# First spread before the second group, a VectorE copy in the last four chunks, and loads and routing queued later

## The chip, the cores and the metric

The kernel runs on one core of a Trainium2 chip. A core has five engines that run side by side, each with its own queue that is worked off in order: TensorE (PE, matrix products into PSUM), VectorE (DVE), ScalarE (ACT), GpSimd (POOL) and SyncE (SP), which here only issues DMA transfers. They wait for each other through semaphores. The metric is the device time of one execution in microseconds (us), as a median of several runs.

## The reference

Two stages follow each other. The first is a delta-rule attention: 4 batches with 8 heads each, 768 steps, head dimension 48. The second is a mixture of 16 experts, chosen in two levels (4 groups of 4), for the 3072 tokens of 384 values that the first stage yields.

```python
k_n = k / (np.linalg.norm(k, axis=-1, keepdims=True) + 1e-06)
for t in range(S):
    y[:, :, t] = einsum('bhd,bhde->bhe', q[:, :, t], state)
    v_old = einsum('bhde,bhd->bhe', state, k_n[:, :, t])
    state = state + bt * einsum('bhd,bhe->bhde', k_n[:, :, t], v[:, :, t] - v_old)
...
g_idx = argmax(x @ w_group)                  # the group, and its softmax weight g_w
e_idx = argmax(xg @ w_expert[g])             # the expert in it, and its weight e_w
h = np.maximum(xg[mask_e] @ w1[g, e], 0.0)
out[tok_idx] = (g_w * e_w)[:, None] * (h @ w2[g, e])
```

## The kernel before

**Chunks and groups.** The 768 steps are cut into 24 chunks `u` of 32 steps. One chunk holds 32 steps of all 4 batches, which are 128 rows. Four chunks form a group `g`. Inside a chunk the recursion is a triangular system; its inverse is worked out for a whole group at once by `inverse(g)` on VectorE, as a long row of small operations: a transpose of the Gram matrix (L279), the norms (L287 to L295, with the twelve-step root and two more steps on GpSimd for every group but the first; then L320 to L328 on VectorE), the elimination (L338 to L366), two large products (L369, L372), and a transpose back into `mt` (L377). `spread` (L388 on ScalarE, once L386 on VectorE) copies `mt` into `mtb` in the form that TensorE needs, two copies for each chunk.

**One chunk.** `advance(u)` is the sequential part. TensorE puts `vh`, the scaled values, into PSUM with a product by the identity (L416) and adds the old state applied to the keys (L422); ScalarE copies the negative as `f` (L426). Meanwhile TensorE applies the state to the queries into `o_ps` (L431). Then come `w_ps` (L439) from `f` and `mtb`, its copy `w` (L442), the state update `s_ps` (L449), its two copies to `s_bd` (L455), and the part of the output inside the chunk (L463, or L468 for chunks 14 and later), copied as `x` (L472). The next chunk's L422 needs `s_bd`. So a chunk is a chain through L422, `f`, `w_ps`, `w`, `s_ps` and `s_bd`.

**What stands beside it.** `gram(u)` (L251) makes the Gram matrices ten chunks ahead. `mask(u)` (L268) and `scale(u)` (L403, which writes `vh`) are VectorE's work for each chunk. `logits(u)` turns `x` by TensorE (L490, copied at L496) and multiplies it with the router's weights (L500, copied as `lg` at L502). `route(r)` takes the logits of four chunks, for the last two groups of two, finds the expert and the place of each token and sorts by products (L621). For the last routing groups VectorE does all of it, for the earlier ones GpSimd a large part.

**What sets the order.** The whole first stage is written under a manual schedule: each engine executes its instructions in the order in which the program issues them. Long tasks (`inverse`, `route`) are generators in a list `behind`; `start(task, share)` adds one, `work(n)` lets each advance by its share of a budget, and `allow(what)` advances those that stopped at a named point (a spread, a sort, the roots, an order for ScalarE). So the position of a call in the main loop decides where an instruction stands in its engine's queue. Loads are issued by SP; a tiny ScalarE copy into the buffer (L696) makes a load wait for that point in ScalarE's queue. The lists `bursts` name these loads for the start.

**The end of the stage.** Expert 0 always comes first; its tokens are gathered before the others (`gather_first`, `add_gathered`, L729), and the tokens of the last four chunks are added to it from memory on the chip (`add_near`, after `only_first`, L742). After a last sort the experts follow: for each, two products (L964 and L983) with weights loaded from memory, until the end.

The order in one turn of the main loop, as far as the change moves it:

```python
next(turned)                    # L785: turn x of the chunk before
work(10)
if u < NCH: allow(SORT)         # L789
next(step)                      # L798: w_ps and its copy
for v in ahead_of[u]: gram(v)   # L799
next(step); next(turned)        # L802: s_ps, s_bd; logits
work(9)
next(step)                      # L818: output of the chunk
work(14)
if u + 1 < NCH: mask(u + 1)     # L829
if u + 2 < NCH: scale(u + 2)    # L831
```

Of the kernel before, what the change touches and what calls it, by code (L numbers as in the profile page):

```python
# [15 lines left out]
C = 32  # L16
RG = 4
SHARE = 0.64
LEAD = 10
FIXED, TILE = 1, 128  # L20
LAST = 8
# [6 lines left out]
def constants(n_tokens, seq, n_experts, n_group, n_batch):  # L28
# [11 lines left out]
                                 .reshape(C, 2 * C) for b in range(n_batch)], axis=0),  # L40
        "tiny": np.full((128, 1), 1e-36),
# [25 lines left out]
def deltanet_then_moe(  # L67
# [109 lines left out]
    with ExitStack() as first:  # L177
# [10 lines left out]
        NB, NV = LEAD + 2, 3  # L188
        kqt_ = [ap_.tile([128, 2, NP, 128], F32, name=f"kqt{i}") for i in range(NB)]
# [28 lines left out]
        def of_kq(u, a=None):  # L218
# [7 lines left out]
            2 * RG + 2: [of_kq(2 * RG), of_kq(2 * RG + 1),  # L226
                         (kv_[2], [lambda: load_kv(2),
                                   lambda: nc.sync.dma_start(out=wr, in_=wr_d)])]
            + [of_kq(u) for u in range(2 * RG + 2, NB)],
        }  # L230
        rooted = sm.tile([128, 1], F32, tag="rooted", name="rooted", bufs=1)
# [32 lines left out]
        def mask(u):  # L264

            like = [128, H, 2, C]
            gqs[u] = wk.tile(like, F32, tag="gqm", name=f"gqm{u}", bufs=3)
            nc.vector.tensor_tensor(  # L268
                gqs[u], raws.pop(u)[:, :, None, :].to_broadcast(like),
                cut["upper"].rearrange("p (a t) -> p a t", a=2)[:, None].to_broadcast(like),  # L270
                op=ALU.mult)
# [138 lines left out]
        def advance(u):  # L410
# [5 lines left out]
            nc.tensor.matmul(a_ps.rearrange("p h d -> p (h d)"), lhsT=ident,  # L416
                             rhs=vh.rearrange("p h d -> p (h d)"), start=True, stop=(u == 0),
                             skip_group_check=True)
            if u > 0:
                for j in range(NP):  # L420
                    for b in range(B):
                        nc.tensor.matmul(a_ps[quads[b], 2 * j:2 * j + 2, :],  # L422
                                         lhsT=kqt[:, 0, j, quads[b]], rhs=s_bd[:, b, j],
                                         start=False, stop=True, skip_group_check=True)
            f = wk.tile([128, H, D], F32, tag="f", name=f"f{u}")
            nc.scalar.activation(f, a_ps, ACT.Copy, scale=-1.0)  # L426
# [32 lines left out]
            for h in range(H):  # L459
# [6 lines left out]
                else:  # L466
                    for b in range(B):
                        nc.tensor.matmul(o_ps[quads[b], h], lhsT=gq[quads[b], hq, b % 2],  # L468
# [217 lines left out]
        with tc.manual_schedule(engines={mybir.EngineType.PE, mybir.EngineType.DVE,  # L686
                                         mybir.EngineType.Activation, mybir.EngineType.Pool,
                                         mybir.EngineType.SP}):
            nc.scalar.activation(rooted, cut["tiny"], ACT.Exp)
            homes = [None, s_ps[:, 0:2], s_ps[:, 2:4]]  # L690
            first_grams = ([(u, (0,)) for u in range(RG)] + [(u, (0, 1)) for u in range(RG, 2 * RG)]
                           + [(u, (1,)) for u in range(RG)])
            for i, (u, parts) in enumerate(first_grams):
                gram(u, homes[i % len(homes)], parts)
                for late, loads in bursts.get(i, ()):
                    nc.scalar.activation(late[:, 0:1], cut["tiny"], ACT.Copy)  # L696
                    for load in loads:
                        load()
# [4 lines left out]
            scale(0)  # L703
            nc.gpsimd.memset(acc[:, 0], 0.0)
# [3 lines left out]
            ahead = advance(0)  # L708
            next(ahead)
            for u in range(2 * RG, LEAD):  # L710
                gram(u, homes[u % len(homes)])
            start(inverse(1), 0.95)
            made = 0
            while 0 not in mts:
                work(4)
                if 1 not in vhs and 0 in turned_over:
                    mask(0)
                    scale(1)
                allow(ACT_STEP)
                made += 1  # L720
                if made == LAST:
                    allow(ROOTS)
            allow(FACTOR)
            ahead_of = {u: [u + LEAD] if u + LEAD < NCH else [] for u in range(NCH + 1)}
            begun, x_in = set(), {}
# [42 lines left out]
            for u in range(NCH + 1):  # L768
                if u == NCH:
                    add_gathered(gathered, [0])  # L770
                step = advance(u) if u < NCH else iter([None] * 4)
                turned = logits(u - 1) if u else iter([None] * 2)
                if u:
# [11 lines left out]
                next(turned)  # L785
                if u:
                    allow(SPREAD)
                work(10)
                if u < NCH:  # L789
                    allow(SORT)  # L790
                if u + 2 == NCH:
                    allow(SORT)
                if u == NCH - 1:
                    for v in near[:2]:
# [402 lines left out]
```

## Time and profile before

| What | Value |
|---|---|
| Median of 3 runs | 515.59 us (514.5 to 517.28) |
| The profiled execution | 511.25 us, of which the span on the engines is 509.0 us |
| First `w_ps` (chunk 0) | starts at 42.49 us |
| First product of chunk 20 that needs the state (L422) | starts at 199.32 us |
| Last logits copy `lg` | starts at 231.52 us |
| First product of the experts (L964) | starts at 238.76 us |
| Mean granted TensorE clock | 0.994 |

The profiled execution is one run of its own; sums over its rows are to be set against its 511.25 us. Times in its views count from the start of the span. A row of the timeline has a start, a length, the engine, the source line, the operation, output and inputs by name, shape and count; in square brackets stands how long the engine was idle before, and what ended that wait. PE busy time is not a measure of TensorE at its peak, since matrix products overlap.

### The profile page before, as it was taken

The numbers are of one execution on the slowest core, as the hardware profiler recorded it, in microseconds if no ns is written. First come the engines' busy times: TensorE is split into PE (matmuls) and PEld (weight loads), VectorE is DVE, ScalarE is ACT, GpSimd is POOL, SyncE is SP. The second block draws the span as 40 slices with busy tenths as digits, with TensorE's granted clock in tenths as the row PEclk, the third lists the DMA queues.
The fourth block names the chain that finished last, engine by engine and source line by source line (L and its number), as shares of the span: only waits on it lengthen the run. The fifth ranks groups of instructions, "written<-read, shape, count | busy, mean of one in ns | idle before, by whom it ended". The sixth has DMA issues, their size and how long they took to land.

```text
span 509.0 us, 18246 instructions
## 1 busy us (share of the span) xinstructions
PE 470.6 (92%) x7844; PEld 437.8 (86%) x7844; DVE 250.3 (49%) x829; ACT 188.9 (37%) x397; POOL 193.7 (38%) x288
## 2 busy tenths in 40 slices
PE   4346999999999999999999999999999999999993
PEld 3235878888888888889999999999999999999992
DVE  3999999999999995527312012102201121011110
ACT  3224768687676767652111111111111211111110
POOL 0040200633806425010445564466435654355231
PEclk9999999999999999999999999999999999999997
DMA  5781434444423546210798788769868978879740
GB/s 178 246 311 40 153 135 157 160 154 158 134 71 117 160 147 198 74 45 17 180 370 249 250 268 269 228 220 331 269 193 282 321 270 260 262 253 310 256 134 26
DMA packets 57333, 99.94 MB, mean 196 GB/s; under 512 B 18974, under 2 KB 41433, under 8 KB 57251
## 3 DMA queue, kind: packets, MB, share of 16 engines
q1 hardware_dynamic: 51331, 88.76, 52.7%
q0 software_dynamic: 5920, 10.00, 6.4%
q8 instruction: 63, 1.03, 0.8%
q14 instruction: 19, 0.16, 0.1%
HBM read 84.61 MB, written 14.27 MB: 194 GB/s over the span
## 4 chain that ended last, share of the span: by engine, by line
PE 57%; DMA 20%; DVE 7%; ACT 5%; SPq 4%; issue 4%; POOL 2%; DVEq 0%; POOLq 0%; ACTq 0%
PE y_ps L983 12%; PE h_ps L964 12%; DMA y_dram<-yq 9%; DMA out_dram<-yo,to_i 5%; PE w_ps L439 5%; PE s_ps L449 5%; DMA yr<-y_dram 5%; PE a_ps L422 3%; SPq L1023 3%; PE l_ps L500 3%; ACT s_bd L455 3%; PE o_ps L463 3%; PE o_ps L431 3%; PE g_ps L251 2%; PE a_ps L416 2%
## 5 line engine op out<-in xcount | busy, mean ns | idle before, releaser
L983 PE MATMUL y_ps<-hid,w 128*128 128x224 f32 (+15 forms) x768 | 132.2, 331 | 0.0
L983 PEld LDWEIGHTS y_ps<-hid,w 128*128 128x128 f32 x768 | 129.0, 190 | 0.3
L964 PE MATMUL h_ps<-xt,w 128*128 128x232 f32 (+14 forms) x720 | 122.7, 330 | 0.0
L964 PEld LDWEIGHTS h_ps<-xt,w 128*128 128x128 f32 x720 | 120.1, 190 | 0.3
L936 POOL DMA_INDIRECT xq<-x_dram,from_q x92 | 87.6, 952 | 36.5 <-issue 24.1
L986 DVE COPY yt<-y_ps 128x232 f32<-128x232 f32 (+13 forms) x14 | 5.1, 366 | 139.7 <-PE y_ps L983 139.7
L967 ACT ACTIVATE hid<-h_ps 128x448 f32<-128x448 f32 (+15 forms) x64 | 32.1, 502 | 100.2 <-PE h_ps L964 100.2
L995 POOL DMA_INDIRECT out_dram<-yo,to_i x32 | 34.1, 1066 | 91.5 <-DVE yo L1033 80.0
L988 ACT ACTIVATE yt<-y_ps 128x224 f32<-128x224 f32 (+15 forms) x34 | 11.5, 337 | 116.6 <-PE y_ps L983 116.6
L360 DVE TENSOR_TENSOR t<-m 128x81 f32<-128x81 f32 (+13 forms) x156 | 51.8, 332 | 0.2
L366 DVE TENSOR_TENSOR m<-m,t 128x81 f32<-128x81 f32 (+13 forms) x156 | 51.4, 330 | 0.0
L455 ACT ACTIVATE s_bd<-s_ps 48x768 f32<-48x768 f32 x46 | 37.0, 805 | 13.9 <-PE s_ps L449 13.3
L343 DVE SCALAR_TENSOR_TENSOR m<-m 128x29 f32<-128x29 f32 (+27 forms) x174 | 40.7, 237 | 0.4
L388 ACT ACTIVATE mtb<-mt,con 128x256 f32<-128x256 f32 x47 | 34.2, 741 | 1.6 <-DVE mt L377 1.5
L1033 DVE TENSOR_SCALAR yo<-yr,gate 128x384 f32<-128x384 f32 (+14 forms) x28 | 11.1, 416 | 43.0 <-DMA yr<-y_dram 35.4
L439 PE MATMUL w_ps<-f,mtb 64*64 64x48 f32 x768 | 28.0, 224 | 3.9 <-DVE mtb L386 3.9
L251 PE MATMUL g_ps<-kqt 48*32 48x64 f32 (+1 forms) x1216 | 18.5, 241 | 13.5 <-issue 8.8
L439 PEld LDWEIGHTS w_ps<-f,mtb 64*64 64x64 f32 x768 | 25.1, 138 | 6.2 <-ACT mtb L388 4.1
L422 PEld LDWEIGHTS a_ps<-s_bd,kqt 128*32 128x32 f32 x736 | 15.3, 111 | 15.5 <-ACT s_bd L455 7.3
L539 POOL TENSOR_TENSOR acc<-acc,hots 128x16 f32<-128x16 f32 x16 | 5.7, 354 | 60.1 <-DVE hots L537 59.1
L251 PEld LDWEIGHTS g_ps<-kqt 48*32 48x32 f32 x1216 | 14.6, 118 | 15.3 <-issue 10.5
L449 PE MATMUL s_ps<-w,kv 32*128 32x96 f32 x736 | 27.4, 286 | 0.1
(159 smaller groups left out, 603.5 us busy)
## 6 DMA issues: line engine op xcount, KB each, us to landing
w<-in_w_dram SPq DMA_DIRECT2D x29, 1536.0 KB
kv<-in_kv_dram SPq DMA_DIRECT2D x24, 448.0 KB, 4.1
kqt<-in_kq_dram SPq DMA_DIRECT2D x20, 512.0 KB, 4.2
x_dram<-x SPq DMA_DIRECT2D x24, 192.0 KB, 2.3
w<-in_w_dram SPq DMA_DIRECT2D x24, 128.0 KB, 3.7
y_dram<-yq SPq DMA_DIRECT2D x36, 84.0 KB, 9.2
yr<-y_dram SPq DMA_DIRECT2D x14, 192.0 KB, 2.5
kqt<-in_kq_dram SPq DMA_DIRECT2D x8, 256.0 KB, 3.5
```

Of the source, the lines that this page charges most:

```text
L251: nc.tensor.matmul(g_out[quads[b], hh * NP + j, of], lhsT=kqt[rows, 0, j, quads[b]], rhs=kqt[rows, of, j, quads[b]], start=True, stop=True ...
L343: nc.vector.scalar_tensor_tensor(row, in0=m[:, j, 0:j], scalar=m[:, i, j:j + 1], in1=row, op0=ALU.mult, op1=ALU.add)
L360: nc.vector.tensor_tensor(tv, m[:, j + 2:, j:j + 1].to_broadcast([128, n, j]), m[:, j:j + 1, 0:j].to_broadcast([128, n, j]), op=ALU.mult)
L366: nc.vector.tensor_tensor(below, below, tv, op=ALU.add)
L388: nc.scalar.activation(mtb[:, rows, a], from_, ACT.Copy, scale=by)
L439: nc.tensor.matmul(w_ps[b, h], lhsT=mt[b, uu * H + (h % 2) * NP + h // 2], rhs=f[b, h], start=True, stop=True, skip_group_check=True)
L449: nc.tensor.matmul(s_at[:, b, j], lhsT=k[quads[b], j], rhs=w[quads[b], 2 * j:2 * j + 2], start=(u == 0 and j == 0), stop=True, skip_group_ ...
L455: nc.scalar.activation(s_bd[rows, :, :, hh, :], s_at[rows, :, :, hh * D:(hh + 1) * D], ACT.Copy)
L936: nc.gpsimd.indirect_dma_start(out=xq[:, g, :], out_offset=None, in_=x_dram[:, :].rearrange("n (q c) -> (n q) c", q=4), in_offset=bass.Ind ...
L964: nc.tensor.matmul(h_ps[:, k], lhsT=w1[:, j, (f + k) * 128:(f + k + 1) * 128], rhs=xt[:, j, 0:R], start=(j == 0), stop=(j == DC - 1), skip ...
L983: nc.tensor.matmul(y_ps, lhsT=w2[:, f, j * 128:(j + 1) * 128], rhs=hid[:, f], start=(f == 0), stop=(f == FC - 1))
L995: put = nc.gpsimd.indirect_dma_start(out=out[:, :], out_offset=bass.IndirectOffsetOnAxis(ap=to[0:P, i:i + 1], axis=0), in_=yo[0:P, :], in_ ...
```

## The change

At the start, the first spread of group 0 is finished before `inverse(1)` is started at all; `mask(0)`, `scale(1)`, `mask(1)`, `scale(2)` and `mask(2)` are issued between the start of that group and the end of its roots. Two products whose result is used nowhere are put before the first `w_ps`. The last loads of the first burst are split: two of them (chunk 10 of keys and queries, chunk 2 of values) wait for the Gram matrix of chunk 8, two (chunk 11 and the router's weights `wr`) for the `w` of chunk 0. GpSimd's three initialisations come after the roots of group 1. In chunk 0 the store of `x` is issued ahead of two loads. `mask(u + 1)` moves from the end of turn `u` to its beginning. For chunks 14 and later the mask is half as wide, and L468 reads it accordingly.

In the last four chunks (20 to 23) the product by the identity is left away, and VectorE computes `f` as minus the product minus `vh`, in one operation. From chunk 19 on, the turning of `x`, the logits and the sorts come after `w_ps`, and later in the turn; a table says how many sorts are allowed at two points of each turn. The routing of the last groups starts only after the `f` of the following chunk. The first block of gathered tokens is added after the second one, before the count `n_ps`.

```diff
-SHARE = 0.64
+SHARE, SORTS = 0.64, [(0, 1), (0, 2), (0, 2), (2, 2), (0, 0)]
...
+        "causal": np.tile(i < k, (n_batch, 1)),
...
+        LATE, FREE = NCH - LEAD, NCH - RG
...
-            2 * RG + 2: [of_kq(2 * RG), of_kq(2 * RG + 1),
-                         (kv_[2], [lambda: load_kv(2),
-                                   lambda: nc.sync.dma_start(out=wr, in_=wr_d)])]
-            + [of_kq(u) for u in range(2 * RG + 2, NB)],
+            2 * RG + 2: [of_kq(2 * RG), of_kq(2 * RG + 1)],
         }
+        after_gram = [of_kq(2 * RG + 2), (kv_[2], [lambda: load_kv(2)])]
+        after_w = [of_kq(2 * RG + 3), (wr[:, 0], [lambda: nc.sync.dma_start(out=wr, in_=wr_d)])]
...
         def mask(u):
...
+            if u >= LATE:
+                gqs[u] = gqm.rearrange("p h a t -> p (h a t)")[:, 0:H * C].rearrange(
+                    "p (h t) -> p h t", t=C)
+                nc.vector.tensor_tensor(gqs[u], raws.pop(u), cut["causal"][:, None, :].to_broadcast(
+                    [128, H, C]), op=ALU.mult)
+                return
...
-            nc.tensor.matmul(a_ps.rearrange("p h d -> p (h d)"), lhsT=ident,
-                             rhs=vh.rearrange("p h d -> p (h d)"), start=True, stop=(u == 0),
-                             skip_group_check=True)
+            if u < FREE:
+                nc.tensor.matmul(a_ps.rearrange("p h d -> p (h d)"), lhsT=ident,
+                                 rhs=vh.rearrange("p h d -> p (h d)"), start=True, stop=(u == 0),
+                                 skip_group_check=True)
...
-            nc.scalar.activation(f, a_ps, ACT.Copy, scale=-1.0)
+            if u < FREE:
+                nc.scalar.activation(f, a_ps, ACT.Copy, scale=-1.0)
+            else:
+                nc.vector.scalar_tensor_tensor(f, in0=a_ps, scalar=-1.0, in1=vh, op0=ALU.mult,
+                                               op1=ALU.subtract)
...
             for u in range(2 * RG, LEAD):
                 gram(u, homes[u % len(homes)])
+                if u == 2 * RG:
+                    begin(after_gram)
+            for _ in range(2):
+                nc.tensor.matmul(s_ps[:, 0, 0:H * D], lhsT=ident, rhs=cut["below"][:, 0:H * D],
+                                 start=True, stop=True, skip_group_check=True)
+            while 0 not in mts:
+                work(4)
+                allow(ACT_STEP)
+            second = inverse(1)
+            start(second, 0.95)
+            while held.get(second) is not ROOTS:
+                work(2)
+            mask(0)
+            scale(1)
+            mask(1)
+            scale(2)
+            mask(2)
+            allow(ROOTS)
+            while held.get(second) is not FACTOR:
+                work(2)
+            allow(FACTOR)
...
-                if u == NCH:
-                    add_gathered(gathered, [0])
                 step = advance(u) if u < NCH else iter([None] * 4)
                 turned = logits(u - 1) if u else iter([None] * 2)
+                if 1 < u < NCH - 1:
+                    mask(u + 1)
...
-                next(turned)
-                if u:
-                    allow(SPREAD)
+                late = FREE - 1 <= u < NCH
+                while late and waiting:
+                    start(*waiting.pop())
+                if not late:
+                    next(turned)
+                    if u:
+                        allow(SPREAD)
                 work(10)
...
                 next(step)
+                if u == 0:
+                    begin(after_w)
+                if late:
+                    next(turned)
+                    allow(SPREAD)
+                    for _ in range(SORTS[u - FREE + 1][0]):
+                        allow(SORT)
...
                 next(step)
+                if late:
+                    next(turned)
+                    for _ in range(SORTS[u - FREE + 1][1]):
+                        allow(SORT)
...
-                    start(route(r), 0.6 if r == NGR - 2 else 1)
+                    if u < NCH:
+                        waiting.append((route(r), 1))
+                    else:
+                        start(route(r), 1)
...
-                if u + 1 < NCH:
-                    mask(u + 1)
-                if u + 2 < NCH:
+                if 0 < u < NCH - 2:
                     scale(u + 2)
...
             add_gathered(gathered, [1], [DC - 1])
+            add_gathered(gathered, [0])
             nc.tensor.matmul(n_ps, lhsT=ones, rhs=acc[:, NCH], start=True, stop=True)
```

## The prediction

> **What bounds the kernel now.** I read the page first (busy shares and slices), then the chain of waits, then busy time by stage, then the waits of VectorE alone, then the timelines of the start and of the last chunks.
>
> ```profile
> PE 470.6 (92%) x7844; PEld 437.8 (86%) x7844; DVE 250.3 (49%) x829; ACT 188.9 (37%) x397; POOL 193.7 (38%) x288
> ```
>
> Over the whole span VectorE (DVE) looks half idle. By stage (start:end, length, busy time of each engine) it does not:
>
> ```profile
> 44.00:100.00 56.00, 55.09 (x1618) 45.85 (x1616) 55.30 (x205) 39.95 (x77) 12.54 (x35) 1.00 0.42 143
> 100.00:160.00 60.00, 59.38 (x1726) 51.14 (x1726) 59.24 (x219) 43.04 (x84) 25.13 (x56) 1.00 0.37 124
> 160.00:196.00 36.00, 35.03 (x1040) 29.74 (x1039) 35.24 (x118) 24.30 (x46) 16.60 (x29) 1.00 0.50 152
> 196.00:222.00 26.00, 25.34 (x724) 22.00 (x727) 10.51 (x42) 17.03 (x34) 4.77 (x5) 1.00 0.31 104
> ```
>
> From 44 to 196 us VectorE is busy 149.8 of 152 us. The waits view of VectorE for that stretch has one line:
>
> ```profile
> DVE what L601 <- POOL cw L575: 0.5, 2, 0.2
> ```
>
> The chain of waits runs through TensorE there, but VectorE never rests, so each of its results comes only a little before its use. That margin is the number this prediction turns on. For chunk 5, vh (L403) ends at 79.48 and its product (L416) starts at 82.03, a margin of 2.55:
>
> ```profile
> 78.93 0.55 DVE L403 TENSOR_TENSOR vh<-kv,normt 128x384 f32<-128x384 f32 x1
> ...
> 82.03 0.91 PE L416 MATMUL a_ps<-vh,con 128*128 128x384 f32 x2
> ```
>
> For the last group, mt (L377) ends at 195.04, ScalarE spreads it from 196.37, and only then copies the state (s_bd):
>
> ```profile
> 193.79 1.25 DVE L377 STREAM_TRANSPOSE mt<-m 128x1024 f32<-128x1024 f32 x1
> ...
> 196.37 1.37 ACT L388 ACTIVATE mtb<-mt,con 128x256 f32<-128x256 f32 x2
> ...
> 197.64 1.63 ACT L455 ACTIVATE s_bd<-s_ps 48x768 f32<-48x768 f32 x2
> ```
>
> At the start, before and around the first w_ps:
>
> ```profile
> 32.25 0.24 POOL L290 TENSOR_TENSOR r<-r 128x32 f32<-128x32 f32 x1 [3.12 <-DVE r L287]
> ...
> 37.52 1.12 POOL L295 TENSOR_SCALAR nrm<-r 128x32 f32<-128x32 f32 x1
> 37.71 0.91 PE L251 MATMUL g_ps<-kqt 48*32 48x64 f32 x41 [3.65 <-issue]
> ...
> 38.68 0.35 DVE L320 RECIPROCAL r<-nrm 128x32 f32<-128x32 f32 x1
> ...
> 42.49 1.95 PE L439 MATMUL w_ps<-f,mtb 64*64 64x48 f32 x32 [3.88 <-DVE mtb L386]
> ...
> 49.91 1.65 PE L416 MATMUL a_ps<-vh,con 128*128 128x384 f32 x2
> ```
>
> GpSimd's 14 root steps take 32.25 to 38.64 and cost VectorE nothing, since it works on group 0 meanwhile. From 238.8 on, TensorE is busy 261.6 of 270.2 us with the experts, so I pass any shift at 238.8 on unchanged.
>
> **What the Trainium skill says.** "TensorE: Matmul & The Clock Gate", Part 1, says that TensorE runs at half clock until a free-running window of about 3.4 us was busy, and falls back after an idle one. The trace agrees on the two rates (the L416 pair takes 1.65 at 49.91, 0.91 later) but needed longer: work is nearly continuous from 42.49 and the rate changes at about 52.0. "Runtime: NRT & Kernel Launch", Instruction fetch mechanics, says instructions come in 16 KiB blocks by DMA; the page shows 63 instruction packets in 1.03 MB, and TensorE's 3.65 us of "issue" ends when the load burst drains. "SBUF — State Buffer", Who interferes with whom, says a VectorE tensor_tensor with both inputs in SBUF and a GpSimd operation that reads SBUF block each other for a whole instruction. The trace agrees: L294 and L295 take 1.13 and 1.12 beside the two 1024-wide products, other root steps about 0.25.
>
> **The change, part by part.** Durations are this profiled execution's (511.25 us with 509.0 of span; the median of the runs is 515.59, so 4.34 is added at the end).
>
> *Start.* Before mt of group 0 VectorE no longer does the group 1 transpose (1.16 from start to next start), its L287 (0.10) and L320 to L328 (0.85): mt comes 2.1 earlier, and mask(0) and scale(1) no longer stand before the spread, so w_ps of chunk 0 can start at about 39.8, not 42.49: 2.7 gained. The later loads let the instruction block through (3.65 of issue down to about 0.7), and the two idle products (2 x 1.65 cold) fit into TensorE's wait. If the clock is up, the cold stretch from 42.49 to 52.0 shrinks by up to 3.9 (w, gram, s, o, a: 9.5 against about 5.6 at the later rates). So TensorE alone would gain 2.7 to 6.6.
>
> *What it costs VectorE.* The second group now starts only after the spread: transpose, L287, then mask(0), scale(1), mask(1), scale(2), mask(2), and then L320 waits for the roots. Those five fill 3 x 0.60 + 2 x 0.47 = 2.74 us. The roots take 4.65 undisturbed (12 steps in 4.05, two of about 0.3). Beside one mask and one scale, groups 2 to 5 took 0.65 to 0.72 longer; five such operations add 0 at the least and 1.7 at the most. Exposed wait w = 0.2 + 4.65 + (0 to 1.7) - 2.74, so 2.1 to 3.8; I take 3.4. Queued behind it is everything VectorE does next.
>
> I walked VectorE's new order with the old start-to-start times (median per shape). Without w: vh of chunks 4 to 14 unchanged, mt of group 1 later by 0.9 (two masks moved ahead of it), mt of group 5 earlier by 1.0 (six masks of 256 instead of 512 columns, about 0.35 against 0.60, less what was moved ahead). With w: vh of chunk 3 is ready at about 65.05, while TensorE wants it at 59 to 61: the start's gain is waited away there. Chunk 5 is later by 3.4 - 2.55 = 0.85. mt of group 5 ends at 195.04 - 1.0 + 3.4 = 197.4, its spread 1.5 later, so s_bd starts at 198.9, not 197.64: **chunk 20 begins about 1.3 late** (0 to 1.7 over the bounds). Masks are issued a step earlier, which removes their own margin (0.9 at chunk 16) from the list.
>
> *Last four chunks.* L416 goes, but it lay in the wait for s_bd (190.95 to 191.9, L422 at 192.02): nothing. VectorE's f: not shown; the nearest are vh (0.55) and a PSUM copy of 384 columns (0.56). I take 0.56 against ScalarE's 0.49; bounds 0.49 and 0.87 (vh beside GpSimd at 196.78). t_ps and sorting move behind w_ps, which then starts 1.6 after L422 instead of 2.3. s_ps follows at 3.35 (w copy 0.49), s_bd at 4.63, next L422 at 6.32 at best. But o_ps 0.81, l_ps 0.78 and two sorts 0.88 now stand between s_ps (1.08) and the next L422, so TensorE ends last: 3.35 + 3.55.
> - Chunk 20: 6.90 against 7.12: -0.22.
> - Chunk 21: plus r_ps 0.43, 7.33 against 8.03: -0.70.
> - Chunk 22: f waits in VectorE's queue behind routing of group 4. Its second part needs rk, which ScalarE makes after s_bd (6.5 after chunk 21's L422), takes 2.58 (211.50 to 214.08), then scale and mask 0.8: f starts at 9.9, wanted at 8.27. The step takes 9.17 against 8.92: +0.25.
> - Chunk 23 to its last lg: routing of group 5 now starts after f, l_ps and only_first queue later; lg ends at about 7.97, before at 8.13: -0.16.
>
> *Tail.* The first gathered block (6 matmuls, 0.86) moves from a gap (228.74) to before n_ps, where TensorE was just in time (L561 done 234.7, products at 234.79): +0.86.
>
> SP and GpSimd: the moved kqt, kv and wr loads are needed 3 us or more after they land, and x_dram going ahead of them is 0.33 of issue; the three GpSimd initialisations (0.1 to 0.7) move behind the roots, and nothing needs them for 50 us; 32 more constant columns add 16 KB to one load: nothing.
>
> Sum: 1.3 - 0.22 - 0.70 + 0.25 - 0.16 + 0.86 = +1.3, so 512.6 profiled and **516.9** as a median.
>
> **Rivals.**
> - *TensorE is the bound and the start is kept* (the chain view speaks for it, VectorE's 98.5% busy against): -6.6 - 0.83 + 0.86 gives 504.7, median 509.0. Chance 0.12.
> - *The margins hold*: w at 2.1, chunk 20 on time, f(22) not late (step 22 then 7.58: -1.34), the gathered block hidden: -2.4, 508.9, median 513.2. For it: root steps beside small operations do run at 0.34. Chance 0.16.
> - *Slower: TensorE cools at chunk 3.* TensorE waits 4 to 6 us for vh(3). If that is an idle window for the clock, the next stretch is cold again and costs 1.5 (one window) to 3.9 (as at 42.49). From a resumption 0.95 before the old one, a loss above 1.8 exceeds chunk 5's 0.85; at 3.9 the lag is 2.95 and stays, as steps 5 to 13 have no slack on TensorE. Chunk 20 starts 2.5 late: +2.5, 513.8, median 518.1; up to +3.1 with w at 3.8. Against: at a slow start the wait is 2 us. Chance 0.24.
> - Forecast: 0.48.
>
> **How the numbers follow.** 0.5% is 2.6 us, about what a measurement of this kernel can tell from no change. Faster by more: 0.12 + 0.4 x 0.16 and 0.02 of the forecast = 0.20. Slower: half of 0.24 and 0.05 of the forecast = 0.17. The rest, 0.63, is same. The range leaves out the kept start and little else: from the margins' 513.2 to the cold case with w at its bound (511.25 + 3.1 + 4.34 = 518.7), widened by about 1 for the scatter of the runs themselves (514.5 to 517.28): 512.5 to 519.8.
>
> **What would show it.** A gap of 2 to 4 us on VectorE before its second L320; w_ps of chunk 0 near 40; a wait of TensorE for vh at chunk 3; slow L416 after it or not; mt of group 5 at 197 or before 195; f of chunk 22 after four `at`; x_ps before n_ps without a gap. Wrong if VectorE shows idle time between 60 and 190, or if chunk 20 begins before 199.

## The result: 1.3% slower, outside the range on the slow side

The changed kernel took 524.54 us (median of 4 runs, 521.30 to 529.70); the kernel before took 516.43 on the same chip (4 runs). The ratio is 1.0132, 95% interval 1.0083 to 1.0181. The forecast was 516.9 with a range up to 519.8, most of the chance on no measurable change. The profiled execution took 521.30 us with a span of 519.1; before it was 511.25 and 509.0.

A ratio leaves out executions over 1.5% above the quickest of the same kernel; in the changed kernel these are the ones with the lowest mean TensorE clock (0.960 here), which the experiments below trace to the kernel itself, so medians over all executions stand beside the ratios there.

### The profile page after: what moved, and what is told of

Its sections match the earlier page's. It is cut to its first block, busy times and chain, and to the rows that moved or that the text cites. A ratio compares the mean times of both kernels' runs of the same rounds, so it can differ in the third digit from the quotient of the medians.

```text
span 519.1 us, 18240 instructions
## 1 busy us (share of the span) xinstructions
PE 477.9 (92%) x7840; PEld 441.8 (85%) x7840; DVE 249.1 (48%) x833; ACT 186.6 (36%) x394; POOL 191.9 (37%) x288
## 4 chain that ended last, share of the span: by engine, by line
PE 52%; DVE 21%; DMA 10%; issue 5%; POOL 5%; ACT 4%; SPq 2%; POOLq 0%; DVEq 0%; ACTq 0%
PE y_ps L1025 18%; PE h_ps L1006 18%; DMA out_dram<-yo,to_i 5%; DVE t L367 5%; DVE m L373 5%; DVE m L350 3%; ACT s_bd L468 3%; PE w_ps L452 3%; PE s_ps L462 2%; DMA yr<-y_dram 2%; PE l_ps L513 2%; PE x_ps L755 2%; PE a_ps L430 1%; DMA y_dram<-yq 1%; PE o_ps L444 1%
## 5 line engine op out<-in xcount | busy, mean ns | idle before, releaser
L468 ACT ACTIVATE s_bd<-s_ps 48x768 f32<-48x768 f32 x46 | 37.0, 803 | 12.1 <-PE s_ps L462 11.5
L297 POOL TENSOR_TENSOR r<-r 128x32 f32<-128x32 f32 x15 | 5.7, 378 | 65.2 <-DVE r L294 64.4
L462 PEld LDWEIGHTS s_ps<-w,kv 32*128 32x128 f32 x736 | 23.2, 186 | 4.2 <-issue 1.6
```

The source lines that it names most:

```text
L462: nc.tensor.matmul(s_at[:, b, j], lhsT=k[quads[b], j], rhs=w[quads[b], 2 * j:2 * j + 2], start=(u == 0 and j == 0), stop=True, skip_group_ ...
L468: nc.scalar.activation(s_bd[rows, :, :, hh, :], s_at[rows, :, :, hh * D:(hh + 1) * D], ACT.Copy)
```

## The profile after

The page's busy shares and its row of TensorE clock in 40 slices (12.98 us each):

```profile
PE 477.9 (92%) x7840; PEld 441.8 (85%) x7840; DVE 249.1 (48%) x833; ACT 186.6 (36%) x394; POOL 191.9 (37%) x288
...
PEclk9999979999999999996999999999999999999998
```

TensorE is busy 7.3 us longer for the same matrix work, less four identity products and plus two idle ones (products whose result nobody reads). The row of clocks points to the reason: before it read 9 up to the last slice, now it has a 7 and a 6. The stages (start:end, length, then busy time of PE, PEld, DVE, ACT and POOL, granted clock, DMA share, GB/s):

```profile
44.00:100.00 56.00, 51.33 (x1432) 41.77 (x1428) 53.41 (x202) 37.60 (x73) 11.54 (x39) 0.94 0.44 148
100.00:160.00 60.00, 58.66 (x1744) 50.07 (x1743) 59.13 (x212) 41.72 (x82) 25.67 (x54) 1.00 0.38 128
160.00:196.00 36.00, 35.04 (x1039) 29.78 (x1038) 35.17 (x130) 24.99 (x48) 18.42 (x36) 1.00 0.46 145
196.00:222.00 26.00, 22.52 (x674) 19.96 (x665) 11.01 (x37) 14.55 (x29) 4.70 (x7) 1.00 0.36 114
```

VectorE is busy 1.9 us less than before in the first row (53.41 against 55.30). Its waits from 44 to 196 us have one new line, 3.1 us for GpSimd's roots:

```profile
DVE r L327 <- POOL nrm L302: 3.1, 1, 3.1
DVE what L614 <- POOL cw L588: 0.5, 2, 0.2
```

What that does to TensorE at chunks 2 and 3 (start, length, instruction, in brackets the idle time before it and what ended it; the last two lines are the same products before):

```profile
58.59 1.14 PE L462 MATMUL s_ps<-w,kv 32*128 32x96 f32 x30
61.14 0.46 PE L462 MATMUL s_ps<-w,kv 32*128 32x96 f32 x2 [1.40 <-issue]
61.52 0.84 PE L513 MATMUL l_ps<-wr,xt 128*128 128x20 f32 x6
62.30 1.14 PE L476 MATMUL o_ps<-w,gqm 64*64 64x48 f32 x32
65.07 1.65 PE L424 MATMUL a_ps<-vh,con 128*128 128x384 f32 x2 [1.64 <-DVE vh L410]
66.65 1.51 PE L430 MATMUL a_ps<-s_bd,kqt 128*32 128x96 f32 x32
...
66.05 0.91 PE L416 MATMUL a_ps<-vh,con 128*128 128x384 f32 x2
66.89 0.87 PE L422 MATMUL a_ps<-s_bd,kqt 128*32 128x96 f32 x32
```

There are two gaps. One of 1.64 is for vh. One of 1.40 the profile marks "issue", which means that TensorE waited for nothing it shows; I call this an instruction-fetch gap, because a packet of 16,384 bytes of instructions landed at 59.80, 1.34 us before the gap ended (the last section has more on this). After them L424 takes 1.65 instead of 0.91 and L430 1.51 instead of 0.87. The windows view of the same place, cut where the trace's record of the granted clock changes:

```profile
57.16:60.57 3.41, 2.57 (x120) 2.26 (x115) 3.41 (x16) 2.10 (x5) 0.00 (x0) 1.00 0.38 137
60.57:63.98 3.41, 2.30 (x40) 2.05 (x40) 3.41 (x13) 2.23 (x4) 0.91 (x3) 1.00 0.37 130
63.98:67.40 3.42, 2.33 (x22) 1.25 (x26) 3.38 (x12) 0.00 (x0) 2.77 (x9) 0.50 0.19 69
67.40:70.81 3.41, 3.41 (x67) 2.80 (x61) 3.30 (x14) 0.98 (x2) 0.88 (x4) 0.50 0.15 24
```

After a window in which TensorE was busy 2.30 of 3.41 us the clock is 0.50 for two such windows. The second fall is in chunks 22 and 23 (after the last dots, the w_ps of chunk 23 before the change):

```profile
218.07 0.84 PE L444 MATMUL o_ps<-s_bd,kqt 128*32 128x96 f32 x32
220.40 1.14 PE L452 MATMUL w_ps<-f,mtb 64*64 64x48 f32 x32 [1.48 <-DVE f L438]
...
228.31 0.32 PE L452 MATMUL w_ps<-f,mtb 64*64 64x48 f32 x4
228.86 0.57 PE L452 MATMUL w_ps<-f,mtb 64*64 64x48 f32 x13 [0.23 <-issue]
229.68 0.33 PE L452 MATMUL w_ps<-f,mtb 64*64 64x48 f32 x4 [0.25 <-issue]
230.41 0.56 PE L452 MATMUL w_ps<-f,mtb 64*64 64x48 f32 x11 [0.40 <-issue]
...
227.82:231.24 3.42, 2.54 (x59) 1.90 (x47) 1.97 (x10) 0.23 (x1) 1.97 (x2) 1.00 0.34 92
231.24:234.65 3.41, 3.39 (x74) 2.92 (x72) 1.58 (x10) 1.56 (x5) 0.00 (x0) 0.50 0.05 18
...
225.33 1.14 PE L439 MATMUL w_ps<-f,mtb 64*64 64x48 f32 x32
```

Here TensorE waits 1.48 us for f of chunk 22, which does nothing to the clock this time, and then w_ps of chunk 23 comes in four pieces. The three gaps between them (0.88 us) are marked "issue" too, but no packet of instructions landed in step with them, so their cause is not shown. The clock stays at 0.50 until 241.48. Lateness against the kernel before, by the first product with the state (L422, now L430) of each chunk, and at the end:

| | chunk 1 | 3 | 4 | 5 | 11 | 13 | 20 | 21 | 22 | 23 | last lg | first h_ps | span |
|---|---|---|---|---|---|---|---|---|---|---|---|---|---|
| us later | -6.26 | -0.24 | 0.74 | 1.55 | 1.68 | 2.63 | 2.42 | 3.43 | 2.92 | 3.36 | 7.25 | 9.02 | 10.0 |

So 2.4 of the 10 us are there when chunk 20 begins, and 5.7 come between chunk 23 and the first expert product, in a stretch of which 10.24 us ran at half clock. The profiled execution of before (511.25) was quicker than each of its four timed runs (514.50 and more), so the table shows more lateness than the medians, which differ by 8.1.

## The experiments

The expectations weigh three theories. CLOCK: TensorE waits a little in new places, its clock falls to half for some windows, and that is most of the loss. LATENESS: VectorE's 3.1 us wait and the late f are the loss in their own length. ORDER: the new order of the last chunks costs by itself. All kernels ran beside the kernel before on the same chip; "clock kept" counts executions whose mean granted clock over the span was 0.985 or more. The profiles show what that means: the clock is low at the very end of every kernel, and each window of 3.4 us at half clock lowers the mean by about 0.003, so a mean of 0.985 still allows two such windows before the end.

| kernel | executions | median us | before, median | ratio, 95% interval | clock kept |
|---|---|---|---|---|---|
| after_again | 6 | 523.19 | 512.94 | 1.0149 (1.0097 to 1.0200) | 1 |
| start_masks | 22 | 515.25 | 513.25 | 1.0049 (1.0030 to 1.0069) | 12 |
| tail_only | 22 | 519.33 | 513.25 | 1.0040 (1.0009 to 1.0071) | 8 |
| tail_fill | 22 | 516.16 | 513.18 | 1.0052 (1.0032 to 1.0073) | 21 |
| fill3 | 22 | 519.39 | 513.25 | 1.0086 (1.0060 to 1.0112) | 5 |
| fill2 | 6 | 518.87 | 513.18 | 1.0104 (1.0064 to 1.0144) | 0 |
| fills | 17 | 516.73 | 513.18 | 1.0074 (1.0050 to 1.0098) | 10 |
| fill_tail | 6 | 523.02 | 513.25 | 1.0183 (1.0130 to 1.0236) | 2 |
| roots_early | 22 | 514.25 | 512.94 | 1.0029 (1.0007 to 1.0050) | 9 |
| front22 | 5 | 518.05 | 512.94 | 1.0085 (1.0065 to 1.0105) | 0 |
| roots_front | 14 | 511.64 | 512.94 | 0.9988 (0.9961 to 1.0016) | 11 |
| rf_warm | 22 | 519.03 | 519.50 | 0.9987 (0.9961 to 1.0013) | 9 |

The kernel before kept its clock in 57 of 59, 35 of 35, 37 of 38 and, beside rf_warm on a chip where all was slower, 21 of 27 executions. Where the clock falls matters as well as how often: two executions of the kernel before with a mean of 0.981 and 0.977 took only 511.16 and 513.63.

### The change in two halves

start_masks is the changed kernel with the last chunks and the tail of before:

```diff
-        LATE, FREE = NCH - LEAD, NCH - RG
+        LATE, FREE = NCH - LEAD, NCH
...
             for u in range(NCH + 1):
+                if u == NCH:
+                    add_gathered(gathered, [0])
...
-                late = FREE - 1 <= u < NCH
```

> The start, the later loads and the halved masks of the change; the last four chunks and the tail as before. CLOCK (the loss of 8 us is mostly two stretches in which TensorE's granted clock is 0.5, one at chunk 3 from 64.0 to 70.8 us and one in the last chunk from 231.2 to 241.5 us, each after a 3.4 us window with too little work for TensorE): the first stretch comes back, the second does not; chunk 20 starts 2.4 us later than before, the last logits 2.4 later instead of 7.25, ratio to before 1.003 to 1.007. LATENESS (VectorE is the bound, its 3.1 us wait for the roots is the loss and the clock is only a companion): the same at chunk 20, +2.4, ratio 1.003 to 1.007. ORDER (the loss is made by the new order of the last chunks alone): 1.000 within 0.002.

tail_only is the reverse: loads, start and masks of before, loop and tail of the change.

```diff
-        LATE, FREE = NCH - LEAD, NCH - RG
+        LATE, FREE = NCH, NCH - RG
...
+            start(inverse(1), 0.95)
+            made = 0
             while 0 not in mts:
                 work(4)
+                if 1 not in vhs and 0 in turned_over:
+                    mask(0)
+                    scale(1)
```

> The start and the masks as before; the last four chunks and the tail of the change (f of chunks 20 to 23 by VectorE without the identity product, routing of groups 4 and 5 behind f, the gathered block behind the routing). CLOCK: TensorE waits 1.5 us for f of chunk 22 and is starved in chunk 23, so a window with little work can come, and the clock is 0.5 in the last chunk; +4 to +7 us, ratio 1.008 to 1.014, if the free-running window falls badly, else as LATENESS. LATENESS: -0.5 + 0.4 + 0.9, so +0.5 to +2, ratio 1.001 to 1.004, full clock throughout. ORDER: nearly the whole loss, 1.010 to 1.014, at full clock.

Both halves lose, so ORDER as the whole loss is out. Each half's times fall into two groups with the clock: tail_only has a median of 513.27 in its 8 executions that kept it, level with the 513.25 of before, and 520.81 in the other 14. In start_masks the groups are 514.46 and 517.78. So the new order of the last chunks costs nothing that can be told in the executions that keep the clock, and those that do not are 7.5 us slower. Of tail_only's forecasts the median, 6.1 above before, fits CLOCK's 4 to 7, and the ratio LATENESS's 1.001 to 1.004. In the profile of tail_only the place is the wait for f of chunk 22 (TensorE busy 1.73 of 3.41 us, then three windows at half clock):

```profile
215.48:218.89 3.41, 3.34 (x98) 3.01 (x85) 2.44 (x12) 2.02 (x6) 0.00 (x0) 1.00 0.19 62
218.89:222.30 3.41, 1.73 (x39) 1.67 (x39) 2.23 (x5) 0.54 (x2) 0.00 (x0) 1.00 0.01 3
222.30:225.71 3.41, 3.41 (x53) 3.15 (x55) 0.00 (x0) 1.10 (x3) 0.00 (x0) 0.50 0.03 5
```

The step from chunk 22 to 23 takes 12.74 us there, against 9.36 in the changed kernel's profile, where that window kept the clock.

The same profile has chunk 20 at 201.52, 2.2 late, though its start is that of before; tail_fill's below has it at 201.52 too. Both were late from chunk 2 on (by 2.08 and 1.65), with a clock that came up at 55.05 and 54.67 us instead of 52.18. So kernels with an unchanged start can be 2 us late at chunk 20 as well, against this execution of before.

In start_masks' profile chunk 3 is no later than in the changed kernel, but another wait appears that the forecast had not: a sort that waits for GpSimd's `at`, which is made after the root steps of a later group and so comes late when VectorE is late.

```profile
135.68 0.65 PE L634 MATMUL s_ps<-mine,at 128*128 128x48 f32 x4 [1.86 <-POOL at L574]
...
134.23:137.65 3.42, 1.97 (x71) 1.87 (x71) 3.29 (x9) 0.33 (x2) 3.00 (x8) 1.00 0.51 158
137.65:141.06 3.41, 3.41 (x86) 3.07 (x67) 3.10 (x11) 1.69 (x4) 2.96 (x6) 0.50 0.02 5
```

Chunk 11 to 12 takes 13.31 us there, before 8.48, and chunk 20 is 6.9 late where 2.4 was forecast; this execution (518.16) is one of the slower of the 22. In the changed kernel's own profile the same wait is 0.79 us and the clock holds:

```profile
135.45 0.65 PE L634 MATMUL s_ps<-mine,at 128*128 128x48 f32 x4 [0.79 <-POOL at L574]
```

### The changed kernel again

> The changed kernel as it is, on this chip, for the distribution of its executions. CLOCK: its times fall into groups by the mean granted clock, as those of start_masks (514.4 at 0.99, 517.7 at 0.98) and tail_only (513.3 at 0.99, 520.6 at 0.98) did; few or none at 0.99, most at 0.98 to 0.96 and 520 to 528; ratio 1.010 to 1.016. LATENESS: one group within 2 us, whatever the clock.

Median 523.19; one execution of six kept its clock and took 516.81, the others 522.06 to 528.42. Its profile has half clock in five stretches (from 42.42, 66.31, 209.67, 223.33 and 240.39 us), at partly other places than the first profile. LATENESS, which expected one group within 2 us, is wrong as an account of the whole.

### Idle work in the waits

If the clock is the loss, TensorE must become quicker by doing more. tail_fill adds three products of con by con to tail_only, in a bank that nobody reads, where TensorE waits for f of chunk 22:

```diff
+                if u == NCH - 2:
+                    fill = ps.tile([128, H * D], F32, tag="g", name="fill")
+                    for _ in range(3):
+                        nc.tensor.matmul(fill, lhsT=ident, rhs=cut["below"][:, 0:H * D],
+                                         start=True, stop=True, skip_group_check=True)
                 if not late:
```

> tail_only (start and masks as before, last chunks and tail changed) with three idle products of 128x128 by 384 columns between o_ps and w_ps of chunk 22, in a free bank of their own, so that they lie inside TensorE's wait of 1.75 us for f and take 1.36 of it. No work is moved or left out; TensorE only does more. CLOCK: most executions keep a clock of 0.99 (tail_only: 9 of 22 at 0.985 or more); the median comes down from tail_only's 519.3 to 512.5 to 514.5. LATENESS and ORDER: the products gain nothing, median 519 to 520.

The products took 2.20 us, not 1.36 (one product is two records in the trace), so they outlast the wait by about 0.3, and still the median falls from 519.33 to 516.16 on the same chip, and 21 of 22 executions keep their clock, against 8 (the expectation counted 9). Neither profile has a fetch gap near this place. The window of the wait is full now:

```profile
218.58 2.20 PE L804 MATMUL fill<-con 128*128 128x384 f32 x6
220.71 1.13 PE L454 MATMUL w_ps<-f,mtb 64*64 64x48 f32 x32
...
218.51:221.93 3.42, 3.42 (x47) 2.22 (x40) 2.43 (x6) 0.04 (x1) 0.00 (x0) 1.00 0.02 4
```

It did not come down to the 512.5 to 514.5 expected: these executions stand 2.8 above tail_only's best group. The profiled one still falls once, at 235.58, and then takes 2.0 us more than before from the last lg to the experts, against 0.35 where the clock holds there; but its executions with a mean clock of 0.993 and more (median 515.4, five of them) are also 2.5 above tail_only's (513.0, six), so most of the cause stays open. The ratios (1.0052 against 1.0040) do not show the gain; the medians and the clock do.

fill3 put three such products ahead of chunk 3's identity product in the changed kernel.

```diff
             a_ps = ps.tile([128, H, D], F32, tag="s", name=f"a_ps{u}")
+            if u == RG - 1:
+                for _ in range(3):
+                    nc.tensor.matmul(a_ps.rearrange("p h d -> p (h d)"), lhsT=ident, ...
```

> The changed kernel with three idle products of 128x128 by 384 columns on TensorE ahead of the identity product of chunk 3, in the bank that it overwrites: they lie in TensorE's wait for vh (1.64 us) and take 1.36 us at full clock. CLOCK: no stretch at 0.5 near 64 to 71 us, chunk 4 starts 2 us earlier than in the changed kernel or at its vh, chunk 5 about 1.0 earlier, chunk 20 about 1.0 earlier; ratio to before 1.010 to 1.012 (the second stretch stays). LATENESS: chunk 5 and 20 where they are in the changed kernel, ratio 1.013.

In its profile they came too late: the clock had fallen at 63.45, after the fetch gap, and at half clock they took 3.61 us from 67.39. Chunk 20 is then 2.2 later than in the changed kernel's profile. Yet the median is 519.39, 6.1 above before, where after_again is 10.3 above it and the first runs 8.1; the ratio, 1.0086, is below what either theory expected. One profile does not tell what the products did in the other executions, so the run decides nothing. fill2 puts them one chunk earlier, ahead of l_ps of chunk 2, in its bank.

```diff
-            l_ps = ps.tile([128, NL], F32, tag="g", name=f"l_ps{u}")
+            l_ps = ps.tile([128, H * D if u == 1 else NL], F32, tag="g", name=f"l_ps{u}")
+            for _ in range(3 if u == 1 else 0):
+                nc.tensor.matmul(l_ps, lhsT=ident, rhs=cut["below"][:, 0:H * D], ...
+            l_ps = l_ps[:, 0:NL]
```

> The changed kernel with three idle products of the same size ahead of l_ps in chunk 2 (at 61.5), that is before the low-work window closes; TensorE waits 1.6 us for vh in the next chunk, so their 1.36 us cost nothing. CLOCK: no fall near 64 to 66 us, L424 of chunk 3 at 0.91 instead of 1.65; chunk 4 starts 1.5 to 2 earlier than in the changed kernel (74 to 74.5), chunk 5 then by VectorE 0.5 to 1.0 earlier; the last chunks still fall, so the median is 1 to 2 below after_again's 523.2. LATENESS: chunk 4 and 5 as in the changed kernel, median 523.

```profile
61.38 2.20 PE L513 MATMUL l_ps<-con 128*128 128x384 f32 x6
63.42 0.74 PE L517 MATMUL l_ps<-wr,xt 128*128 128x20 f32 x6
64.09 1.14 PE L476 MATMUL o_ps<-w,gqm 64*64 64x48 f32 x32
65.15 0.91 PE L424 MATMUL a_ps<-vh,con 128*128 128x384 f32 x2
```

Chunk 3 begins where it did (65.15 against 65.07) and now runs at full clock: chunk 4 at 75.33 (76.07 in the changed kernel, 0.74 earlier, half of what CLOCK expected) and chunk 5 at 83.59 (0.84 earlier). The fetch gap of 1.40 is not there any more either, so this profile does not tell which of the two kept the clock. And the gain does not last: the sort of chunk 11 now waits longer for `at`, and chunk 12 is 2.13 late, as in the changed kernel (2.18).

```profile
135.40 0.65 PE L638 MATMUL s_ps<-mine,at 128*128 128x48 f32 x4 [1.20 <-POOL at L578]
```

So VectorE's lateness, handed on through GpSimd, sets the time there; the fall at chunk 3 costs nothing that is left at chunk 20 in these profiles. The median, 518.87, is lower than the 521 to 522 expected, with six executions between 515.9 and 527.8. Both sets together, fills:

> The changed kernel with both sets of idle products, six in all; nothing moved or left out. CLOCK: the changed kernel's lateness remains (2.4 at chunk 20, the wait at chunk 22), its low-clock stretches mostly go; median 515 to 518, against 523.2 without the products. LATENESS and ORDER: 523 to 525.

Median 516.73 of 17, 10 with the clock kept, inside the 515 to 518 of CLOCK. That is 3.6 above before, where the changed kernel was 10.3 above it in after_again (6 executions on another chip) and 8.1 in the first runs: 4.6 to 6.7 us less, by six idle products. What the six move besides, above all the places of fetch gaps, is not held apart here; for the last chunks tail_fill does that. The 2.7 at chunk 20 remain, as LATENESS has them.

fill_tail, the first try at the last chunks, put three products ahead of w_ps of chunk 22 and two ahead of that of chunk 23, in the bank of w_ps.

```diff
             w_ps = ps.tile([128, H, D], F32, tag="s", name=f"w_ps{u}")
+            for _ in range({NCH - 2: 3, NCH - 1: 2}.get(u, 0)):
+                nc.tensor.matmul(w_ps.rearrange("p h d -> p (h d)"), lhsT=ident, ...
```

> The changed kernel with idle products of 128x128 by 384 columns ahead of w_ps, in the bank that it overwrites: three in chunk 22 (in TensorE's wait of 1.5 us for f) and two in chunk 23. CLOCK: no stretch at 0.5 between 228 and 242 us, last logits 3 to 4 us earlier than in the changed kernel, ratio to before 1.004 to 1.008. LATENESS and ORDER: the products only cost, up to 0.9 us in chunk 23, ratio 1.013 to 1.016.

That bank comes free with f itself, so the products stood behind the wait and only cost:

```profile
225.11 2.20 PE L451 MATMUL w_ps<-con 128*128 128x384 f32 x6 [1.48 <-DVE f L438]
```

Ratio 1.0183, above what all three theories had for it. In its profile the clock holds from 228 to 242 us, as CLOCK said, but the last lg is 11.6 late instead of 7.25: the wait of 1.48 is still there, the products come on top, and half clock at 65.94, 137.62 and 205.89 had cost time before. The run was no test of the theories.

### Taking the waits away

roots_early starts the second group ahead of mt of group 0, so that its transpose and first root step stand there again (1.35 us of VectorE) and GpSimd makes the roots meanwhile.

```diff
-            while 0 not in mts:
-                work(4)
-                allow(ACT_STEP)
             second = inverse(1)
             start(second, 0.95)
+            while 0 not in mts:
+                work(4)
+                allow(ACT_STEP)
             while held.get(second) is not ROOTS:
```

> The changed kernel with one thing moved back: the second group's transpose and its first root step (L286, L294; 1.35 us of VectorE) stand before mt of group 0 again, so that GpSimd makes the roots beside the end of group 0. First w_ps 1.3 later (40.3), VectorE's wait of 3.1 before L327 gone, vh of chunk 3 ends near 62 instead of 65, no wait of TensorE for it. LATENESS: chunk 5 and chunk 20 3.1 earlier than in the changed kernel (chunk 20 at 198.6), time 3.1 lower, one group. CLOCK: the same at chunk 20 and besides no stretch at 0.5 before 130 us; the low-clock stretches of the last chunks stay, in a half to two thirds of the executions as in tail_only; median 516 to 519, its best executions near 511.

VectorE's wait is gone, L424 of chunk 3 starts without one, and chunk 20 starts at 198.62, as both theories had it to the digit.

```profile
65.19 0.91 PE L424 MATMUL a_ps<-vh,con 128*128 128x384 f32 x2
```

The median is 514.25, 8.9 below after_again's on the same chip: three times the wait that was removed, and lower than CLOCK's 516 to 519 too. CLOCK had no fall before 130 us; the profile has one, from 42.02 to 52.26, which leaves no lateness at chunk 3, and another from 205.86. The 9 executions that kept their clock (513.98) are hardly quicker than the other 13 (514.82), so here the mean clock does not sort the times.

front22 moves t_ps and two sorts of chunk 22 ahead of its w_ps again (1.5 us of work into the wait of 1.5).

```diff
+                if u == NCH - 2:
+                    next(turned)
+                    for _ in range(2):
+                        allow(SORT)
                 if not late:
                     next(turned)
```

> The changed kernel with chunk 22's transposes (t_ps) and two sorts (1.5 us of TensorE work) ahead of its w_ps again, where TensorE waits 1.5 us for f. ORDER and LATENESS: 1.4 us lower than the changed kernel and no more. CLOCK: the window around 218 to 221 us is filled, so fewer executions fall to 0.5 in the last chunks: median 3 to 5 us lower than the changed kernel (ratio to before 1.004 to 1.008), the first stretch at chunk 3 stays.

Median 518.05, 5.1 below after_again's, at the edge of CLOCK's 3 to 5, and 1.4 was LATENESS's and ORDER's. Five executions, all between 517.3 and 518.7, none of them with the clock kept. The profile has half clock at 66.03 and 137.71 but not in the last chunks. Both edits, roots_front:

> Both of the former edits. CLOCK: hardly a stretch at 0.5 left before the experts; most executions at a mean clock of 0.99 or above, ratio to before 0.995 to 1.002. LATENESS: 4.5 below the changed kernel, ratio 1.004.

Median 511.64 against 512.94, ratio 0.9988 with an interval that holds 1. The page's clock row:

```profile
PEclk9999999999999999999999999999999999999998
```

This profiled execution has a span of 507.9; its chunk 20 starts 1.02 before that of the kernel before, its last lg 1.63, and w_ps of chunk 23 comes in one piece.

```profile
223.41 1.14 PE L452 MATMUL w_ps<-f,mtb 64*64 64x48 f32 x32
```

The 11.6 us between after_again and roots_front are thus two waits of 3.1 and 1.5 us with what hung on them.

rf_warm adds a third idle product at the start of roots_front.

```diff
-            for _ in range(2):
+            for _ in range(3):
                 nc.tensor.matmul(s_ps[:, 0, 0:H * D], lhsT=ident, rhs=cut["below"][:, 0:H * D],
```

> roots_front with three idle products instead of two in TensorE's wait before the first w_ps: one more at half clock takes 1.65 us, the wait there is 1.70. CLOCK: from 35.3 to 44.2 us TensorE is busy without a gap, which holds a whole window of 3.4 us, so the clock is full by about 42 instead of 50.0 and chunk 1 starts about 3 us earlier than in roots_front (47.0 against 50.0). Whether that is kept tells the bound of the stretch behind it: if TensorE is (start kept), chunk 20 starts 2 to 3 earlier and the time is 2 to 3 lower, ratio 0.993; if VectorE is, chunk 4 to 6 wait for vh or mtb, chunk 20 stays within 0.5 of roots_front's 198.3, ratio 0.997 to 1.000, with more executions fallen to half clock if the new waits are long.

The ratio is 0.9987, that of roots_front within the error, and of the two cases the one of VectorE as the bound. In the profile (an execution of 522.30, the median is 519.03) the clock was full from 39.83, but a fetch gap of 1.53 us at 43.0 brought it down again from 46.66 to 50.07, so chunk 1 started at 48.69, not 47.0, and a second fetch gap of 1.2 us brought the clock down at 63.73. Chunk 20 started at 201.84, not within 0.5 of 198.3. Whether a kept start would last to chunk 20 stays open. No version clearly beats the kernel before.

## Why the prediction was wrong

By the steps of the prediction:

- *Start.* Right. w_ps of chunk 0 at 39.02 (39.8 forecast); the two idle products did bring the clock up, full from 40.09 in this execution, and chunk 1 began 6.26 earlier (2.7 to 6.6). Not in each: in after_again's profile it fell again from 42.42 to 49.25.
- *VectorE's wait for the roots.* Right: 3.07 (3.4 forecast). vh of chunk 3 was ready at 65.02 (65.05).
- *Chunk 5 and chunk 20.* 1.55 and 2.42 late, 0.85 and 1.3 forecast, and not by the path that was forecast. vh of chunk 5 was there at 82.54, 1.04 before its product began; 0.84 of chunk 5's lateness is absent in fill2, at full clock. From chunk 5 to 13 another 1.1 came, 0.8 of it the sort that waits for GpSimd's `at`, which the walk of VectorE's order alone did not hold. mt of group 5 ended at 196.95 (197.4), but chunk 20 did not wait for it: chunks 13 to 19 were already 2.6 late, and its spread began only at 198.16, behind two other copies of ScalarE, as it did at 197.94 in tail_only, where that mt was there at 195.58. That chunk 20 still came within 1.1 us of its forecast is luck.

```profile
197.77 0.49 ACT L509 ACTIVATE xt<-t_ps 128x384 f32<-128x384 f32 x1
198.16 1.36 ACT L395 ACTIVATE mtb<-mt,con 128x256 f32<-128x256 f32 x2
```

- *Chunks 20 to 22.* Chunk 20's step took 8.13, not 6.90: the order of its parts is as computed, but L481 stands still 0.96 us in a fetch gap. Chunk 21: 7.52 (7.33). Chunk 22: f started 9.92 after chunk 21's products (9.9), the step took 9.36 (9.17).
- *Chunk 23 to the last lg.* This is the step that failed: 12.0 us against 7.97 forecast. The sum took every product of TensorE here at full clock and without a gap; the profile has 0.88 us of gaps in w_ps and then half clock, which by difference makes about 3.2 (an estimate). With the clock full and no gap it takes 8.0 in roots_front.
- *Tail.* Last lg to h_ps 9.01, before 7.24: 1.77 late against 0.86, partly at half clock. Where the clock holds there, as in roots_front, roots_early, front22 and fills, the gathered block costs 0.35. The experts themselves took another 1.0 in this execution and not in the experiments but rf_warm; no cause was sought.

Most times of waits were right to a few tenths, and the sum was wrong: 1.3 was forecast, and this profile is 10.0 late. Of the 8.7 between them, 4.0 lie in chunk 23, 1.2 in chunk 20's step, 1.1 before chunk 20, 0.9 in the tail, 1.0 in the experts and 0.4 in chunks 21 and 22. So what the sum left out is that TensorE's clock can fall behind a wait or a gap in the last chunks, and that such gaps come without any wait; both were put at nothing there without a reason given. "TensorE cools at chunk 3" was a rival, with a chance of 0.24 and 518.1 us, and the fall came; but it was applied to one place, and to the one where, by fill2, it did not matter in the end. The prediction had itself computed that f of chunk 22 comes 1.6 us late, booked 0.25 for it, and did not ask what the gap does to the clock. Nor did it ask where instruction blocks end once matmuls are added or removed. The rival was also held to need a long gap. The Trainium skill, "TensorE: Matmul & The Clock Gate", Part 1, has the clock fall after an idle window; the windows ahead of this kernel's two falls were busy for 67 and 74%.

## What to carry to other kernels

Where TensorE runs without a gap, price a new wait by what it does to the clock, not by its length alone: here taking away waits of 1.5 and 3.1 us brought about 5 and 9 us, and 11.6 together. Look for the places where an edit leaves TensorE underfed for a window of 3.4 us, whether by a wait or by instruction fetch, and move work that is needed anyway into them (transposes, sorts), or idle products at the least. When times of one kernel fall into groups, sort them by the granted clock before comparing medians, and then look where in the kernel it fell: in roots_early a fall of three windows at the start left no lateness at chunk 3.

## What the runs showed of the hardware

The clock changes on a grid. In the changed kernel's profile the stretches between changes last 6.83, 160.43 and 10.24 us, that is 2, 47 and 3 windows of 3.413 us; the same page of the skill gives that window and says that it runs freely, which fits: places move between executions of the same kernel. How little is enough, this case can tell. I laid this grid over the profiles of before, after and the twelve experiments, and took from the matmul records how busy TensorE was in each window at full clock that began between 36 and 490 us:

| busy share of the window | windows | followed by half clock |
|---|---|---|
| under 0.60 | 16 | 13 |
| 0.60 to 0.70 | 11 | 9 |
| 0.70 to 0.80 | 25 | 6 |
| 0.80 to 0.85 | 27 | 1 |
| 0.85 and more | 1703 | 0 |

The share doesn't decide alone: the window at 217.58 of the changed kernel, 57% busy, kept its clock, and one of 82% in fill_tail lost it. What else decides was not found. Once low, the clock stayed so for one to four windows, at times (fill3, from 223.87) through four in which TensorE was busy without a gap.

The same fourteen profiles say what the fetch gaps are. Between 30 and 250 us TensorE has 73 gaps over 0.15 us that are marked "issue". 67 of them end 1.2 to 1.6 us after a packet of 16,384 bytes of the instruction queue has landed; the other six are those inside w_ps of chunk 23 in the changed kernel and in rf_warm.
